# How far the row maxima run ahead, how they are turned, and where the hash bits stand in the matrix stream

## The chip, the cores and the metric

The kernel runs on one core of a Trainium2 chip. It is one program and one launch; the other cores are idle. The metric is the device time of one execution in microseconds, the median of several runs. A profiled execution is taken beside them; its trace gives every instruction of the engines: TensorE (PE, with its weight loads as PEld), VectorE (DVE), ScalarE (ACT), GpSimd (POOL), and the issues of transfers on SyncE's queue (SP).

## The reference

Two parts follow each other: attention over hash buckets, and a feed-forward layer.

```python
q_bits = (einsum('bhsd,dk->bhsk', q, proj) > 0)     # 6 bits; the same for k
mask = q_bucket[:, :, :, None] == k_bucket[:, :, None, :]
scores = where(mask, scale * q @ k.T, -1e9)
attn = exp(scores - max(scores)); attn /= sum(attn) + 1e-9
x = (attn @ v) arranged as [4*768, 8*64]
h = x @ w_in                                         # 512 -> 2048
g = where(h >= 1, h, where(h <= -1, 0, (h + 1)**2 / 4))
out = g @ w_out                                      # 2048 -> 512
```

There are 4 batches of 8 heads, 768 positions and head width 64, all in float32. A query and a key may only meet if all six signs of their projections agree.

## The kernel before, in words

**Pairs and phases.** Two heads make a pair; there are 16 pairs. Queries are handled in halves of 384 columns, so attention is a sequence of 32 phases: phase 2p is the first half of pair p, phase 2p+1 its second. A phase has six score steps (`s_step`, lines 324 and 328), one for each block of 128 keys. A step computes the transposed scores of both heads into a slot of PSUM (three products for the precision, line 324, and one with the mask rows, line 328), and ScalarE writes their exponentials (line 330). At the end of the phase come the output products with the values (`pv_group`, line 375, two groups of three key blocks) and the sums of the exponentials over the keys: GpSimd adds three blocks each (`sum_part`, line 339), and four small products with ones finish the sum of the phase before (`sum_mm`, line 349, into the bank aux; `sum_put` copies it on ScalarE, line 362, and stores it).

**Mask rows.** For each pair the tile `MB` holds rows of the hash bits. The product of these rows over queries and keys (line 251 and line 328) adds a large negative number where bits differ. One more row holds, for each query, the negated maximum of its scores, so that line 328 also subtracts the maximum. The hash bits of pair p+2 are made in one of pair p's phases: `bits_mm` (line 211, four products of 32 output rows into one bank), `bits_cmp` (VectorE), `bits_scale` (ScalarE), and `bits_put`, eight small transfers on SP's queue (line 238).

**Maxima.** The row maximum must be known before the phase that needs it. So each phase also computes untransposed scores of later phases: a maximum (`max_mm`, lines 248 and 251) is one block of 128 queries against half of the keys, for both heads, into a slot; `max_red` (line 261) reduces it on VectorE into a column of a tile `nr`. Six maxima make one phase's rows. Phases 1 to 6 do seven each, so from phase 7 on the maxima run a full phase further ahead than at the start.

**Turning.** The maxima stand in columns and are needed as a row. There are two ways. `row_first` (line 290, six products of 97 output rows, a copy on ScalarE, two one-row operations on VectorE, line 300) stands between the two groups of output products; it serves the rows of phases 1 to 7. `half_turn` (line 268, four products of 67 output rows in the 64-row shape that the maxima have) stands behind the sixth maximum of a phase; `half_put` takes the smaller of both halves on VectorE (line 277) and sends the row into `MB` with two transfers on SP's queue (line 283), and a copy to memory with two more (line 285). It serves phases 8 to 31, in the phase ahead of each.

**Order.** All order is written by hand: an engine runs its instructions in program order. A string gives the order of maxima (M) and score steps (s) within a phase and the slot of each; `PLAIN` outside of phases 8 to 26, `CLOSE` within. Slots 0 to 2 have two banks each; a fourth is made of the output bank and aux.

```python
PLAIN = "MMsMsMsMsMss", (0, 1, 2, 3, 0, 1, 2, 3, 0, 1, 2, 0)
CLOSE = "MMsMssMsMsMs", (0, 1, 2, 3, 0, 1, 2, 0, 3, 1, 2, 0)
```

Work at the end of a phase is collected in bursts by place: 0 and 1 before the output products, 3 between their two groups, 2 behind them. In phases 3 to 26 VectorE and ScalarE also prepare weights for the second part there (lines 69 to 82), with a bank of slot 1 as scratch. SP's queue is in order too: it issues each transfer once what it waits for is done. In phases 28 to 31 VectorE and GpSimd prepare the first columns of x for the feed-forward layer (lines 634 to 639), and in phases 30 and 31 VectorE does the additions of line 339 as well.

**Feed-forward.** From 408.9 us on, PE computes the two matrix products (lines 757, 894 and 989); the change doesn't touch that part.

Of the kernel before, what the change touches and what calls it, by code (L numbers as in the profile page):

```python
# [25 lines left out]
NJ = S // P  # L26
# [85 lines left out]
ADDS = (0, 1, 3, 4)  # L112
DIRECT, VSUM = 1, 58
AHEAD0 = (0, 2, 3, 4, 5, 6)
AT = 5
WORD, TURN, TFIRST = 1, 2, True
PLAIN = "MMsMsMsMsMss", (0, 1, 2, 3, 0, 1, 2, 3, 0, 1, 2, 0)
CLOSE = "MMsMssMsMsMs", (0, 1, 2, 3, 0, 1, 2, 0, 3, 1, 2, 0)
C0, C1 = 8, 27
# [2 lines left out]
def order(ph):  # L122

    return CLOSE if C0 <= ph < C1 else PLAIN


def turns(ph, kind):

    return [t for x, t in zip(*order(ph)) if x == kind]


def ahead(ph, j):

    seen = [i for i, x in enumerate(order(ph)[0]) if x == "s"]
    return order(ph)[0][:seen[j]].count("M")
# [3 lines left out]
def attention(ctx, tc, wst, T1, T2, qk, v, pj, cv, x_d, s_d, n_d, tasks, shared):  # L139
# [6 lines left out]
    slots = [psum.tile([P, 2, 512], F32, name=f"s{i}") for i in range(3)]  # L146
    obank = psum.tile([P, 512], F32, name="o")
    aux = psum.tile([P, 512], F32, name="aux")
    shared["word"] = slots[WORD][:, 0].bitcast(I32)
    slots = [[t[:, 0], t[:, 1], t] for t in slots] + [[obank, aux]]  # L150
# [92 lines left out]
    def max_mm(pr, i, kh, ps):  # L243
        qr, mb = QR(pr), MB(pr)
        its = slice(i * P, (i + 1) * P)
        smax[pr, i, kh] = ps
        for h in range(2):
            nc.tensor.matmul(out=ps[h][:, 0:HS], lhsT=qr[64 * h:64 * h + 64, 0, its],  # L248
                             rhs=qr[64 * h:64 * h + 64, 1, halves[kh]], start=True, stop=False)
        for h in range(2):  # L250
            nc.tensor.matmul(out=ps[h][:, 0:HS], lhsT=mb[64 * h:64 * h + 33, 0, its],  # L251
                             rhs=mb[64 * h:64 * h + 33, 1, halves[kh]], start=False, stop=True)

    def max_red(pr, i, kh):
        hf = i // NG
        nr = NR[(2 * pr + hf) % 3]
        ps = smax.pop((pr, i, kh))
        c = 32 + i % NG
        for o, x in ([(nr[:, kh, c::64], ps[2][:, :, 0:HS])] if len(ps) > 2
                     else [(nr[:, kh, c + 64 * h:c + 64 * h + 1], ps[h][:, 0:HS]) for h in range(2)]):  # L260
            nc.vector.tensor_reduce(out=o, in_=x, axis=AX.X, op=ALU.max, negate=True)  # L261

    def half_turn(pr, hf, ps):
        nr = NR[(2 * pr + hf) % 3]
        for kh in range(2):
            for h in range(2):
                r = slice(64 * h, 64 * h + 64)
                nc.tensor.matmul(out=ps[h][0:TW, HS + 64 * kh:HS + 64 * kh + 64], lhsT=nr[r, kh, 32:32 + TW],
                                 rhs=ident_r[r, r], start=True, stop=True, skip_group_check=True)
        te = small.tile([TW, P], F32R, name="te")  # L270
        halfs[pr, hf] = te, ps[2][0:TW, :, HS + 64:HS + P]
        nc.scalar.copy(out=te.rearrange("p (h n) -> p h n", h=2), in_=ps[2][0:TW, :, HS:HS + 64])

    def half_put(pr, hf):
        te, other = halfs.pop((pr, hf))
        tv = te.rearrange("p (h n) -> p h n", h=2)
        nc.vector.scalar_tensor_tensor(out=tv, in0=tv.bitcast(F32), scalar=CLAMP, in1=other, op0=ALU.min, op1=ALU.min)
        b, sl = 2 * pr // H, halves[hf]
        for o in (None, n_d[b]):
            for h in range(2):  # L280
                t = te[64 * h:64 * h + NG].bitcast(F32)
                if o is None:
                    nc.sync.dma_start(out=MB(pr)[64 * h + 7:64 * h + 8, 0, sl].bitcast(F32), in_=t)
                else:
                    nc.sync.dma_start(out=o[2 * pr % H + h:2 * pr % H + h + 1, sl], in_=t)
# [48 lines left out]
    def sum_part(gr, n):  # L334
        p = [PT[(NG * gr + i) % NP_][:, :, 0:HS] for i in range(NG)]
        eng = nc.vector if gr >= VSUM else nc.gpsimd
        if n == 0:
            sums[gr] = work.tile([P, 2, HS], F32, name="part", bufs=2)
        eng.tensor_tensor(out=sums[gr], in0=sums[gr] if n else p[0], in1=p[n + 1], op=ALU.add)  # L339
# [11 lines left out]
    def sum_last(gr):  # L351

        for i in range(NG):
            for k in range(2):
                for h in range(2):
                    r = NW * (2 * h + k)
                    nc.tensor.matmul(out=aux[r:r + NW, 0:HS], lhsT=ones, rhs=pts[NG * (gr + k) + i][:, h, 0:HS],
                                     start=(i == 0), stop=(i == NG - 1), skip_group_check=True)
# [33 lines left out]
    def keep_rows(n):  # L392

        for _ in range(n):
            for h in range(2):
                r = slice(64 * h, 64 * h + 64)
                nc.tensor.matmul(out=(obank, aux)[h][:, 0:2 * P], lhsT=idle[r, 0:P], rhs=idle[r],
                                 start=True, stop=True)
# [59 lines left out]
    events, mids, bursts = defaultdict(list), defaultdict(list), defaultdict(list)  # L458

    def burst(ph, place, fn, *a):  # L460
        bursts[ph, place].append((fn, a))
# [9 lines left out]
    k = 0  # L471
    last, halves_of = {}, {}
    for ph in range(NPH):
        for m in range(7 if 0 < ph < 7 else NJ):
            q, i = 1 + k // NJ, k % NJ
            if q < NPH:
                events[ph].append((q // 2, q % 2 * NG + i // 2, i % 2, slots[turns(ph, "M")[m] if m < NJ else WORD]))
                last[q] = ph
            k += 1
    for q in range(1, NPH):  # L480
        ph = last[q]
        if ph == q - 1:
            burst(ph, 3, row_first, q // 2, q % 2, slots[TURN])
        else:
            halves_of[ph + 1] = q // 2, q % 2
    for pr in range(NPAIR):
        if pr + 2 < NPAIR:
            if pr > 0:
                mids[NU * pr - 4].append((load_qk, (pr + 2,)))
            ph = 2 * pr + (pr == 0)  # L490
            burst(ph, 0, bits_mm, pr + 2)
            burst(ph, 1, bits_cmp, pr + 2)
            burst(ph, 1, bits_scale, pr + 2)
            burst(ph, 1, bits_put, pr + 2)
            for t in range(2):
                burst(ph, 1, round_qk, pr + 2, t)
                mids[NJ * ph + NJ + 2 + 2 * t].append((low_qk, (pr + 2, t)))
        if pr + 1 < NPAIR:
            mids[NU * pr + 3].append((load_v, (pr + 1,)))

    def run(l):
        for fn, a in l:
            fn(*a)

    made = defaultdict(int)

    def maxima(ph, upto):
        while made[ph] < min(upto, max(NJ if ph in halves_of else 0, len(events[ph]))):
            m = made[ph]
            made[ph] += 1  # L510
            turned = m == AT and ph in halves_of
            if m < len(events[ph]):
                a = events[ph][m]
                max_mm(*a)
                if turned:
                    half_turn(*halves_of[ph], a[3])
                max_red(*a[:3])
            elif turned:
                half_turn(*halves_of[ph], slots[turns(ph, "M")[m]])
            if turned:  # L520
                half_put(*halves_of[ph])

    NF_ = NS // NJ
    for ph in range(NF_ + 1):
        for j in range(NJ):
            n = NJ * ph + j
            if n < NS:
                maxima(ph, ahead(ph, j) if ph else AHEAD0[j])
                if n == 1:
                    keep_rows(4)  # L530
                s_step(n)
                if n == 0:
                    keep_rows(4)
            if 0 < ph < NF_ - DIRECT + 1 and j in ADDS:
                k = ADDS.index(j)
                sum_part(2 * ph - 2 + k // 2, k % 2)
            run(mids.pop(n, ()))
            if j < NJ - 1:
                for k in range(2):
                    run(tasks.pop(2 * n + k, ()))  # L540
        maxima(ph, NJ + 1)
        run(bursts.pop((ph, 0), ()))
        run(bursts.pop((ph, 1), ()))
        run(tasks.pop(2 * (NJ * ph + NJ - 1), ()))
        if NF_ - DIRECT <= ph < NF_:
            sum_last(2 * ph)
            sum_put(2 * ph)
        if ph < NF_:
            pv_group(2 * ph)
            run(bursts.pop((ph, 3), ()))  # L550
            pv_group(2 * ph + 1)
        if TFIRST:
            run(bursts.pop((ph, 2), ()))
        if 0 < ph < NF_ - DIRECT + 1:
            sum_mm(2 * ph - 2)
            sum_put(2 * ph - 2)
        run(bursts.pop((ph, 2), ()))
        run(tasks.pop(2 * (NJ * ph + NJ - 1) + 1, ()))
    assert not bursts and not pts and not sums, (events, bursts)
    for g in sorted(tasks):  # L560
# [659 lines left out]
```

## Time and profile before

| | us |
|---|---|
| median of 3 runs | 926.98 (926.97 to 927.6) |
| profiled execution | 927.48 |
| span of its trace | 925.7 |
| PE busy | 917.5 |
| DVE busy | 666.4 |
| ACT busy | 524.9 |
| POOL busy | 313.2 |
| first product of the feed-forward layer | 408.90 |

The granted clock of TensorE is 1.000 through the whole span. A busy PE isn't PE at its peak, since the ends of matmuls are modelled; what counts is the distance between the starts of its instructions. The profiled execution's time is its span and 1.8 us around it.

### The profile page before, as it was taken

To read this page: it belongs to the slowest core of one execution; us is meant where nothing else is said; L and a number is where in the kernel's file an instruction comes from. 1 tells how busy PE (TensorE), PEld (TensorE's weight loads), DVE (VectorE), ACT (ScalarE), POOL (GpSimd) and SP (SyncE) were. 2 spreads that over 40 slices of the span, in tenths; PEclk is the share of its full clock that TensorE was granted. 3 is DMA by queue.
4 is the path that set the end of the run, shared out by engine and by line. 5 is a ranking of instruction groups with operands and counts; after the bars stand their busy time and mean duration, and the time that the engine had idled before them with its cause. 6 is when DMAs were issued, how large, how long until landed. Compare 5 with 4: busy or idle time off the path is not lost.

```text
span 925.7 us, 17069 instructions
## 1 busy us (share of the span) xinstructions
PE 917.5 (99%) x6217; PEld 733.1 (79%) x6217; DVE 666.4 (72%) x1167; ACT 524.9 (57%) x895; POOL 313.2 (34%) x222
## 2 busy tenths in 40 slices
PE   9999999999999999999999999999999999999998
PEld 6667766666666666669999888889889889888986
DVE  6578877777777776849987877876857777655564
ACT  4556666666666665546565555464654545644444
POOL 5588788777878888640000000000000000000000
PEclk9999999999999999999999999999999999999999
DMA  2233334444444433553944789865395654644421
GB/s 89 93 120 132 119 115 139 145 142 142 146 145 141 143 124 102 147 150 133 318 165 137 249 275 292 268 184 158 105 265 150 187 149 122 186 114 116 124 80 68
DMA packets 91412, 142.96 MB, mean 154 GB/s; under 512 B 14288, under 2 KB 53056, under 8 KB 91328
## 3 DMA queue, kind: packets, MB, share of 16 engines
q1 hardware_dynamic: 91040, 141.87, 49.7%
q8 instruction: 49, 0.80, 0.4%
q14 instruction: 35, 0.29, 0.1%
q10 hardware_dynamic: 288, 0.01, 0.0%
HBM read 106.23 MB, written 34.06 MB: 152 GB/s over the span
## 4 chain that ended last, share of the span: by engine, by line
PE 95%; DVE 2%; ACT 1%; DMA 1%; SPq 1%; issue 0%; ACTq 0%; DVEq 0%
PE y L757 28%; PE h L989 19%; PE o L375 14%; PE s L324 11%; PE h L894 7%; PE s L328 3%; PE s L248 3%; PE aux L349 2%; PE s L251 2%; PE aux L211 1%; PE o L248 1%; PE o L251 1%; PE s L290 1%; PE aux L390 0%; DVE nr L261 0%; DMA t<-ed 0%
## 5 line engine op out<-in xcount | busy, mean ns | idle before, releaser
L330 ACT ACTIVATE p<-s 128x768 f32<-128x768 f32 x192 | 155.5, 814 | 59.7 <-PE s L328 55.8
L261 DVE TENSOR_REDUCE nr<-s 128x2 fp32r<-128x768 f32 x132 | 123.2, 956 | 77.2 <-PE s L251 52.1
L722 DVE SCALAR_TENSOR_TENSOR t<-t 128x384 f32<-128x384 f32 x128 | 71.3, 557 | 103.5 <-ACT z L717 103.4
L375 PE MATMUL o<-p,vraw 128*64 128x384 f32 (+1 forms) x768 | 132.8, 491 | 0.0
L339 POOL TENSOR_TENSOR part<-p,p 128x768 f32<-128x768 f32 x58 | 107.1, 1846 | 68.1 <-PE aux L349 67.8
L757 PE MATMUL y<-t,ghi 128*128 128x512 f32 x384 | 124.6, 395 | 0.5 <-ACT ghi L727 0.5
L375 PEld LDWEIGHTS o<-p,vraw 128*64 128x64 f32 x768 | 51.6, 136 | 69.1 <-issue 64.6
L339 POOL TENSOR_TENSOR part<-part,p 128x768 f32<-128x768 f32 x58 | 98.4, 1696 | 3.6
L324 PE MATMUL s<-t,t 64*128 64x384 f32 x768 | 98.4, 333 | 0.0
L727 ACT CAST ghi<-z 128x384 fp32r<-128x384 f32 x129 | 65.1, 505 | 29.9 <-DVE z L723 26.1
L989 PE MATMUL h<-wbig,t 128*128 128x384 f32 x399 | 81.4, 336 | 0.0
L717 ACT ACTIVATE z<-t,m 128x384 f32<-128x384 f32 x128 | 79.0, 617 | 4.2
L757 PEld LDWEIGHTS y<-t,ghi 128*128 128x128 f32 x384 | 71.3, 188 | 11.7 <-ACT ghi L727 0.9
L716 ACT ACTIVATE t<-h,mh 128x384 f32<-128x384 f32 x56 | 32.6, 582 | 83.9 <-PE h L894 45.9
L757 PE MATMUL y<-t,glo 128*128 128x512 f32 x192 | 76.0, 396 | 0.0
L757 PE MATMUL y<-woh,glo 128*128 128x512 f32 x192 | 75.7, 394 | 0.2
L989 PEld LDWEIGHTS h<-wbig,t 128*128 128x128 f32 x399 | 71.6, 188 | 5.2
L757 PE MATMUL y<-woh,ghi 128*128 128x512 f32 x192 | 75.5, 393 | 0.0
L757 PE MATMUL y<-wol,ghi 128*128 128x512 f32 x192 | 75.5, 393 | 0.0
L723 DVE TENSOR_TENSOR z<-t,z 128x384 f32<-128x384 f32 x128 | 71.4, 558 | 4.6
L324 PE MATMUL s<-t 64*128 64x384 f32 x384 | 71.1, 365 | 1.2 <-ACT p L330 0.9
L731 DVE TENSOR_TENSOR glo<-z,ghi 128x384 fp32r<-128x384 f32 x128 | 70.5, 550 | 0.2 <-ACT ghi L727 0.2
(192 smaller groups left out, 1815.2 us busy)
## 6 DMA issues: line engine op xcount, KB each, us to landing
t<-wc SPq DMA_DIRECT2D x92, 256.0 KB
wraw<-wc SPq DMA_DIRECT2D x76, 256.0 KB
qk<-in_qk_dram SPq DMA_DIRECT2D x15, 768.0 KB
wraw<-in_w_in_dram SPq DMA_DIRECT2D x16, 512.0 KB
wraw<-in_w_out_dram SPq DMA_DIRECT2D x16, 512.0 KB
t<-ed SPq DMA_DIRECT2D x36, 192.0 KB
xd<-xs SPq DMA_DIRECT2D x16, 385.0 KB
vraw<-in_v_dram SPq DMA_DIRECT2D x16, 384.0 KB
```

The source lines that it names most:

```text
L261: nc.vector.tensor_reduce(out=o, in_=x, axis=AX.X, op=ALU.max, negate=True)
L324: nc.tensor.matmul(out=ps[h][:, 0:HS], lhsT=k[r, 1, ks], rhs=q[r, 0, sl], start=(k is hi and q is hi), stop=False)
L330: nc.scalar.activation(out=p[:, :, 0:HS], in_=ps[2][:, :, 0:HS], func=AF.Exp, scale=SCALE)
L339: eng.tensor_tensor(out=sums[gr], in0=sums[gr] if n else p[0], in1=p[n + 1], op=ALU.add)
L375: nc.tensor.matmul(out=obank[64 * h:64 * h + 64, 0:w], lhsT=vraws[pr][:, j, h, :], rhs=p[:, h, 0:w], start=(j == 0), stop=(j == NJ - 1), s ...
L717: nc.scalar.activation(out=z, in_=t, func=AF.Relu, scale=1.0, bias=m1)
L722: nc.vector.scalar_tensor_tensor(out=t, in0=t, scalar=1.0, in1=t, op0=ALU.min, op1=ALU.mult)
L723: nc.vector.tensor_tensor(out=z, in0=t, in1=z, op=ALU.add)
L727: nc.scalar.copy(out=g[0], in_=g[2])
L731: nc.vector.tensor_tensor(out=g[1], in0=g[2], in1=g[0].bitcast(F32), op=ALU.subtract)
L757: nc.tensor.matmul(out=ys[c][m], lhsT=g_[:, m * P:(m + 1) * P], rhs=w, start=(first and k == 0), stop=(last and k == 2))
L989: nc.tensor.matmul(out=ps, lhsT=w[:, cs], rhs=x, start=(n == 0 and s not in (2, 3, 6)), stop=(n == 5), skip_group_check=True)
```

## The change

Four things are edited.

- The maxima: phases 1 to 3 do seven, all others six (`LEADS = 3`). So three are done ahead rather than six, and phase 30, which had none, does the last three.
- The turning: `row_first` serves phases 1 to 3 only; from the row of phase 4 on `half_turn` is used. In phase 3 it stands behind the seventh maximum (`at_of`), elsewhere behind the sixth place as before.
- The hash bits: from phase 4 on `bits_mm` stands behind the output products and directly ahead of the row sums, and writes the second bank of slot 2 in place of aux. `bits_cmp`, `bits_scale` and `bits_put` follow it there (place 4). The rounding of the pair's queries and keys stays where it was.
- The switch `TFIRST`, which has no use any more, is gone, and where no maximum is left to share a slot with, the turn takes slot 1 (`WORD`).

```diff
-AT = 5
-WORD, TURN, TFIRST = 1, 2, True
+LEADS = 3
+WORD, TURN, HASH = 1, 2, 2
...
-        for m in range(7 if 0 < ph < 7 else NJ):
+        for m in range(NJ + (0 < ph <= LEADS)):
...
-        ph = last[q]
-        if ph == q - 1:
-            burst(ph, 3, row_first, q // 2, q % 2, slots[TURN])
+        if q > 3:
+            halves_of[q - 1] = q // 2, q % 2
         else:
-            halves_of[ph + 1] = q // 2, q % 2
+            burst(last[q], 3, row_first, q // 2, q % 2, slots[TURN])
...
-            burst(ph, 0, bits_mm, pr + 2)
-            burst(ph, 1, bits_cmp, pr + 2)
-            burst(ph, 1, bits_scale, pr + 2)
-            burst(ph, 1, bits_put, pr + 2)
+            burst(ph, 2 * (ph > 2), bits_mm, pr + 2, slots[HASH][1] if ph > 2 else aux)
+            for fn in (bits_cmp, bits_scale, bits_put):
+                burst(ph, 4 if ph > 2 else 1, fn, pr + 2)
...
+    def at_of(ph):
+
+        return NJ if ph <= LEADS else NJ - 1
+
     def maxima(ph, upto):
-        while made[ph] < min(upto, max(NJ if ph in halves_of else 0, len(events[ph]))):
+        while made[ph] < min(upto, max(at_of(ph) + 1 if ph in halves_of else 0, len(events[ph]))):
             m = made[ph]
             made[ph] += 1
-            turned = m == AT and ph in halves_of
+            turned = m == at_of(ph) and ph in halves_of
...
             elif turned:
-                half_turn(*halves_of[ph], slots[turns(ph, "M")[m]])
+                half_turn(*halves_of[ph], slots[WORD])
...
-        if TFIRST:
-            run(bursts.pop((ph, 2), ()))
+        run(bursts.pop((ph, 2), ()))
+        run(bursts.pop((ph, 4), ()))
         if 0 < ph < NF_ - DIRECT + 1:
             sum_mm(2 * ph - 2)
             sum_put(2 * ph - 2)
-        run(bursts.pop((ph, 2), ()))
```

## The prediction

> **What bounds the kernel now.** I read the page's busy shares and its chain of waits first, then the places of the output products (line 375, one stretch per phase) in that chain, and last the timelines of TensorE, VectorE, ScalarE and the DMA queue around one hash phase and around phases 29 to 31.
>
> ```profile
> PE 917.5 (99%) x6217; PEld 733.1 (79%) x6217; DVE 666.4 (72%) x1167; ACT 524.9 (57%) x895; POOL 313.2 (34%) x222
> PE 95%; DVE 2%; ACT 1%; DMA 1%; SPq 1%; issue 0%; ACTq 0%; DVEq 0%
> ```
>
> The matrix engine is busy 99% of the span and makes up 95% of the chain. So an edit counts by what it takes from PE's stream or by a hole that it puts into it; idle time elsewhere is free. Phase lengths can be read from the chain as the distance between successive line 375 rows (the first of each phase):
>
> ```profile
> 77.69 2.09 PE o L375 x12
> ...
> 90.45 2.10 PE o L375 x12
> ...
> 104.00 2.08 PE o L375 x12
> ...
> 116.42 4.04 PE o L375 x24
> 128.86 4.02 PE o L375 x24
> 140.50 4.04 PE o L375 x24
> ```
>
> These are phases 4 to 9. Up to phase 6 the products are cut in two (x12) by a row turn; from phase 7 on they are whole (x24). Phase 5 lasts 90.45 - 77.69 = 12.76 us and phase 6 13.55 (it holds hash products, phase 5 doesn't). Phase 7 has 12.42, phase 8 (hash) 12.44, phase 9 (none) 11.64.
>
> **Part 1: rows in row tiles, one maximum fewer.** Phases 4 to 6 lose their seventh maximum and their row turn and get the small turn that phases 8 and 9 have already. So phase 5 should come to phase 9's length (12.76 - 11.64 = 1.12) and phases 4 and 6 to phase 8's (13.55 - 12.44 = 1.11 each): 3.34. Phase 7 loses the row turn that phase 6 had left in its interval: 12.42 - 11.64 = 0.78. Phase 3 keeps seven maxima and gains a small turn, which takes
>
> ```profile
> 127.04 0.25 PE L268 MATMUL s<-ident_r,nr 64*67 64x64 f32 x4
> ```
>
> 0.25 us at most, so -0.2. Together 3.34 + 0.78 - 0.2: **3.9 us** less in the first eight phases. Each turned row also brings three more transfers (four instead of one) on SP's queue in phases 3 to 6 and takes two one-row VectorE operations away; neither is on the path there. In phase 3 ScalarE's copy of the turned rows stands behind two exponentials and the weight operations of VectorE behind it, in the bank of the next phase's second maximum; PE's output products (4.0 us) cover that, about to the tenth. If the cover fails it costs a few tenths once.
>
> **Part 2: hash products between output products and row sums** (12 phases, 4 to 26).
>
> ```profile
> 128.01 0.85 PE L211 MATMUL aux<-qk,pw 128*32 128x384 f32 x8
> 128.79 4.09 PE L375 MATMUL o<-p,vraw 128*64 128x384 f32 x24
> 132.81 0.85 PE L349 MATMUL aux<-part,ones 128*32 128x384 f32 x8
> 133.59 0.45 PE L248 MATMUL s<-t 64*128 64x384 f32 x2
> ...
> 134.05 0.34 PE L248 MATMUL s<-t 64*128 64x384 f32 x2
> ...
> 134.41 0.34 PE L324 MATMUL s<-t 64*128 64x384 f32 x2
> ...
> 135.12 0.34 PE L248 MATMUL o<-t 64*128 64x384 f32 x1
> ...
> 402.00 2.14 PE L357 MATMUL aux<-p,ones 128*32 128x384 f32 x24
> 404.07 1.19 PE L375 MATMUL o<-p,vraw 128*64 128x386 f32 x6
> ```
>
> Hash products and row sums have one shape (128 rows, 32 columns). Alone, eight instructions of it cost 0.78 (128.01 to 128.79), and the hash phase is 12.44 - 11.64 = 0.80 longer. The last sums put 24 of them in a row: 2.07, so each further eight cost (2.07 - 0.78) / 2 = 0.645. Put next to the sums, the hash should cost 0.645: 0.155 x 12 = 1.9 saved. The row's bank and weights don't change between its groups, as here they would, so the lower end is nothing saved; a loss has no row, because the stream loses one change of shape and gains none. I take **1.6**, near the row of the same shape.
>
> The new order adds waits. VectorE's compare now waits for the end of the hash products; behind it are only the next phase's first reductions, which come later anyway. Bank 1 of slot 2 must be free of the compare before the next phase's first scores (134.41, some 1.6 after the hash ends; the compare and its hand-over take 0.7). ScalarE's copy of the row sums now stands behind the scaling of the bits, and frees aux for the third maximum (135.12):
>
> ```profile
> 128.95 0.55 DVE L216 TENSOR_SCALAR bits<-aux 128x384 fp32r<-128x384 f32 x1
> ...
> 129.53 0.71 ACT L219 ACTIVATE bits<-bits,cvt 128x384 fp32r<-128x384 f32 x1 [0.54 <-DVE bits L216]
> ...
> 133.80 0.48 ACT L362 COPY rows<-aux 128x384 f32<-128x384 f32 x1 [0.35 <-PE aux L349]
> ```
>
> In phase 8 the products would start at 128.01 and last 4.02; hash until 132.9, compare and scale until 134.3, the copy until 134.8, against 135.0: hidden, with 0.2 to spare. Without that it would cost a tenth or two per hash phase.
>
> **Part 3: three maxima move to phase 30.** One costs 134.41 - 134.05 = 0.36; three are contained in part 1's gain and come back here.
>
> ```profile
> 380.87 4.11 PE L375 MATMUL o<-p,vraw 128*64 128x386 f32 x24
> ...
> 385.69 0.44 PE L324 MATMUL s<-t 64*128 64x384 f32 x2
> ...
> 386.83 0.44 PE L328 MATMUL s<-t 33*128 33x384 f32 x1 [0.19 <-DMA t<-te]
> ...
> 391.79 4.09 PE L375 MATMUL o<-p,vraw 128*64 128x384 f32 x24
> ```
>
> Phase 30 has no maxima before, and PE has holes in it: 0.3 for a row's transfer (386.83) and about as much twice for exponentials. The maxima (1.08) would fill these and cost 0.3 if that were all. But the small turn for phase 31 needs the reductions of these maxima, which until now were done a phase earlier, and VectorE has its own work in front:
>
> ```profile
> 385.86 1.37 DVE L339 TENSOR_TENSOR part<-p,p 128x768 f32<-128x768 f32 x1 [0.81 <-PE aux L349]
> 387.15 0.54 DVE L637 TENSOR_TENSOR qk<-qk,t 128x384 f32<-128x384 f32 x1
> 387.73 0.36 DVE L639 CAST t<-qk 128x384 fp32r<-128x384 f32 x1
> ...
> L261 DVE TENSOR_REDUCE nr<-s 128x2 fp32r<-128x768 f32 x132 | 123.2, 956 | 77.2 <-PE s L251 52.1
> ```
>
> First maximum done 386.4, two reductions of 0.96, a sum (1.37 in its row; I allow 0.95, as the reduction of as many elements), 0.54, 0.36 and the third reduction in two halves (0.96): 391.0, where PE would be there at 390.0. Turn, two scores and change take 1.7: products at 392.7 to 393.0 instead of 391.79. **+1.1**, bounds +0.3 (reductions in time) and +2.0 (another 0.9 on VectorE, as its 1.37 shows possible).
>
> **Part 4: what the hash rows push back on SP's queue.** No term of the diff, but the one that worries me most.
>
> ```profile
> 131.37 5.46 SPq L238 DMA_DIRECT2D t<-bits  x8
> ...
> 138.03 0.37 SPq L187 DMA_DIRECT2D qk<-in_qk_dram  x1
> ...
> 141.51 1.45 SPq L283 DMA_DIRECT2D t<-te  x2
> ...
> 162.11 0.37 SPq L187 DMA_DIRECT2D qk<-in_qk_dram  x1
> ```
> ```profile
> 143.00:144.00 1.00, 1.00 (x8) 0.43 (x6) 0.80 (x2) 0.00 (x0) 1.00 (x1) 1.00 0.78 212
> ...
> 166.00:167.00 1.00, 1.00 (x8) 0.43 (x6) 0.93 (x3) 0.05 (x1) 1.00 (x2) 1.00 0.93 381
> 167.00:168.00 1.00, 1.00 (x8) 0.43 (x6) 0.80 (x2) 0.00 (x0) 1.00 (x1) 1.00 0.06 19
> ```
> ```profile
> 146.58 0.34 PE L328 MATMUL s<-t 33*128 33x384 f32 x2
> ...
> 170.64 0.34 PE L328 MATMUL s<-t 33*128 33x384 f32 x2
> ```
>
> Eight hash rows hold SP for 5.46 us; behind them are the stores and loads of a weight block and a pair, and then the turned row (te) that the next even phase's first line 328 needs. Part 2 lets the hash rows start at 134.3 instead of 131.37, so all behind them comes 2.95 later. The loads, which kept the DMA engines busy (next to last column) until about 143.8 and 167.0, then end at 146.7 and 169.95. The row itself is ready at 141.5 and is now issued behind loads that are still moving. How long it takes with idle engines:
>
> ```profile
> 384.25 1.55 SPq L283 DMA_DIRECT2D t<-te  x2
> 386.40:386.50 0.10, 0.10 (x3) 0.00 (x0) 0.10 (x1) 0.00 (x0) 0.01 (x1) 1.00 0.06 15
> ```
>
> its second half moves at 386.45 and PE goes on at 386.83, nearly 0.4 later. If the row can't pass the loads, it lands at 147.1 in phase 9 and 170.3 in phase 11; it is needed at 146.45 and 170.5 (0.13 earlier than before by part 2). So 0.6 late in phases 9, 17 and 25, which load sums too, and just in time in the eight other odd phases. If it passes them, nothing is late. I take **+1.5**; bounds 0 and 11 x 0.6 = 6.6.
>
> The Trainium skill (DMA: Bandwidth & Descriptors, section "Queues, rings and completion order") has a rule that speaks against the change here: each DMA engine consumes the descriptors of a ring in order, so a small row would stay behind a large load of its queue. By that rule part 4 is paid; without it the sum below would be 1.5 better. No row here shows a row waiting behind loads, or passing them.
>
> **Sum.** -3.9 - 1.6 + 1.1 + 1.5 = -2.9. The profiled execution took 927.48 us (925.7 span and 1.8 around it), 0.5 above the median of 926.98; 927.48 - 2.9 = 924.6 in its terms, and **924.1** as a median.
>
> **Rivals.**
> - *Rows are never late* (part 4 is nothing): -4.4, 922.6. For it: the even margins of 0.2; against: the loads ahead in the one queue, some five microseconds of it.
> - *A little late everywhere*: at 0.4 in each of the 11 odd phases the gain is eaten: -4.4 + 4.4, 927.0. The eight phases with 0.2 to spare are near enough.
> - *Hash gains nothing and phase 30 pays 2.0*, so the change moves work without its main effect: -3.9 + 2.0 + 1.5, 926.6. For it: VectorE's slow operations around 385; against: line 357's row.
> - *Slower: the turned row stuck behind the loads.* Place: the first line 328 of each even phase. Price 0.6 in all 11, 6.6: -4.4 + 6.6 = +2.2, 929.2. It decides from 0.4 per phase on, which needs loads 0.6 slower than 167.0 shows, or a DMA engine that lags behind the mean share.
>
> **How the numbers follow.** 0.2% is 1.85 us, about what a measurement of this kernel can tell from no change. Forecast 40% (923 to 925.1), never late 20%, a little late 14%, hash nothing 14%, slower 12%. Faster 0.60, same 0.28, slower 0.12. The range for eight in ten is 921.6 (parts 2 and 3 at their good ends, nothing late: -3.9 - 1.9 + 0.3 = -5.5) to 927.8 (the two cases near no change with the measurement's spread); the forecast's own is 923 to 925.1.
>
> **What would show it.** Part 1: line 290 falls from 42 to 18 instructions and line 268 rises from 96 to 112; phases 4 to 7 by the chain near 12.3, 11.6, 12.3, 11.6. Part 2: from the hash row to the sums 0.65, hash phases 12.3. Part 3: products of phases 29 and 30 some 12 apart, and a wait of line 268 for the reductions. Part 4: line 328 waiting for te in phases 10, 18 and 26. The forecast is wrong if even phases show that wait throughout, or none, or if line 248's third maximum waits for ScalarE's copy.

## The result, and the profile after

The changed kernel takes 931.67 us (five executions, 929.87 to 933.18) against 926.97 for the kernel before (926.53 to 927.6). The ratio is 1.0051 with an interval of 1.0035 to 1.0067: it is slower by 4.7 us, where I had forecast 2.9 less. The profiled execution took 933.18 us, 931.4 of them span (925.7 before).

First the lines of the changed kernel's page that answer to those shown of before: busy times, the chain's shares by engine, and one group of instructions.

```profile
PE 917.2 (98%) x6209; PEld 734.9 (79%) x6209; DVE 664.3 (71%) x1164; ACT 521.9 (56%) x895; POOL 312.5 (34%) x222
PE 85%; DMA 7%; SPq 3%; DVE 3%; ACT 1%; issue 1%; ACTq 0%; DVEq 0%
L328 PE MATMUL s<-t 33*128 33x384 f32 x384 | 72.7, 340 | 6.1 <-DMA t<-te 5.6
```

PE is no less busy in microseconds (917.2 against 917.5), but its share of the chain falls from 95% to 85%; DMA and SP's queue now hold 10%. The last line says what for: line 328 waits for the turned row (`t<-te`). These waits are listed again under PE's weight loads, since a weight load stands ahead of each product; the two figures are one wait and are not added. Before, TensorE waited for such a row once, 0.2 us at 386.83.

The chain of waits of the changed kernel, from the products of phase 4 to the row for phase 10, and the products of phase 26 (start, length, what ran):

```profile
75.68 4.02 PE o L375 x24
89.54 5.41 DMA t<-te
...
141.61 3.64 DMA t<-te
...
289.12 4.78 DMA t<-te
...
349.44 4.02 PE o L375 x24
```

A turned row's transfer stands in the chain once ahead of each even phase from 6 to 26, eleven times. It takes 3.2 to 5.4 us from its issue to its landing (3.6 to 5.4 in the rows shown), and PE's next product begins as it lands. So the row of each even phase comes late, not three of eleven.

Around one of these, phases 8 and 9, TensorE does this (start, length, instruction, tile, shapes, count, wait in brackets):

```profile
125.82 4.09 PE L375 MATMUL o<-p,vraw 128*64 128x384 f32 x24
129.84 0.85 PE L211 MATMUL s<-qk,pw 128*32 128x384 f32 x8
130.51 0.83 PE L349 MATMUL aux<-part,ones 128*32 128x384 f32 x8
131.27 0.44 PE L248 MATMUL s<-t 64*128 64x384 f32 x2
...
143.89 0.51 PE L324 MATMUL s<-t,t 64*128 64x384 f32 x4
145.29 0.62 PE L328 MATMUL s<-t 33*128 33x384 f32 x2 [0.89 <-DMA t<-te]
```

The first four lines show that the hash move itself did what it was to do: from hash to sums 0.67, from sums to the next shape 0.76, together 1.43 where the two took 0.78 each before. The last two show what it cost: line 328 begins 1.4 us after the four products of line 324 begin, instead of 0.35 (before, 146.23 and 146.58).

SP's queue in the same stretch, and what the DMA engines did (next to last column: their mean busy share):

```profile
132.09 5.45 SPq L238 DMA_DIRECT2D t<-bits  x8
...
138.74 0.37 SPq L187 DMA_DIRECT2D qk<-in_qk_dram  x1
...
141.61 1.46 SPq L283 DMA_DIRECT2D t<-te  x2
```
```profile
144.00:145.00 1.00, 0.40 (x6) 0.08 (x2) 1.00 (x2) 0.11 (x1) 1.00 (x2) 1.00 0.58 137
```

The hash rows go out 6.3 us after the output products begin, then the pair (768 KB) and right behind it, at 139.17, the weight block (512 KB), then the row (two transfers of 1.5 KB). A share of 0.58 in this stretch means that the engines are full until about 144.6, and the row lands at 141.61 + 3.64 = 145.25.

Phase 30, which got the three maxima:

```profile
395.81 0.25 PE L268 MATMUL s<-ident_r,nr 64*67 64x64 f32 x2 [0.63 <-DVE nr L261]
```
```profile
385.79 4.04 PE o L375 x24
...
397.54 4.02 PE o L375 x24
```

The turn's second half waits for the reductions, and the phase takes 397.54 - 385.79 = 11.75 instead of 10.92.

### The profile page after: what moved, and what is told of

It reads as the page before. It is cut to its first block, busy times and chain, and to the rows that moved or that the text cites. A ratio compares the mean times of both kernels' runs of the same rounds, so it can differ in the third digit from the quotient of the medians.

```text
span 931.4 us, 17037 instructions
## 1 busy us (share of the span) xinstructions
PE 917.2 (98%) x6209; PEld 734.9 (79%) x6209; DVE 664.3 (71%) x1164; ACT 521.9 (56%) x895; POOL 312.5 (34%) x222
## 4 chain that ended last, share of the span: by engine, by line
PE 85%; DMA 7%; SPq 3%; DVE 3%; ACT 1%; issue 1%; ACTq 0%; DVEq 0%
PE y L758 28%; PE h L990 18%; PE o L375 10%; PE s L324 8%; PE h L895 7%; DMA t<-te 5%; PE s L328 3%; PE s L248 2%; PE s L251 2%; PE aux L349 1%; SPq L238 1%; PE s L211 1%; DMA t<-ed 1%; PE o L251 1%; DVE nr L261 1%
## 5 line engine op out<-in xcount | busy, mean ns | idle before, releaser
L324 PE MATMUL s<-t,t 64*128 64x384 f32 x768 | 102.1, 333 | 0.0
L328 PE MATMUL s<-t 33*128 33x384 f32 x384 | 72.7, 340 | 6.1 <-DMA t<-te 5.6
L324 PE MATMUL s<-t 64*128 64x384 f32 x384 | 74.7, 364 | 0.7 <-ACT p L330 0.4
```

The costliest lines, as they stand in the source:

```text
L324: nc.tensor.matmul(out=ps[h][:, 0:HS], lhsT=k[r, 1, ks], rhs=q[r, 0, sl], start=(k is hi and q is hi), stop=False)
L328: nc.tensor.matmul(out=ps[h][:, 0:HS], lhsT=mb[r, 1, ks], rhs=mb[r, 0, sl], start=False, stop=True)
```

## The experiments

The theory after the result: parts 1 to 3 brought about what I had worked out, and the late row alone makes the kernel slower. The hash rows, moved behind the output products, push the pair's and the weights' loads back on SP's queue, and the row behind them can't land before they end. Its rivals: the row is late because its issue is late (a matter of the instructions ahead of it on SP, not of their bytes); or the cause isn't the hash move at all, but the maxima or the turn.

**The change without the hash move.** Lines 490 to 492 get back the places and the bank of before; the rest stays as changed.

```diff
-            burst(ph, 2 * (ph > 2), bits_mm, pr + 2, slots[HASH][1] if ph > 2 else aux)
+            burst(ph, 0, bits_mm, pr + 2)
             for fn in (bits_cmp, bits_scale, bits_put):
-                burst(ph, 4 if ph > 2 else 1, fn, pr + 2)
+                burst(ph, 1, fn, pr + 2)
```

> The changed kernel with the hash products, compare, scaling and hash rows back at their old place (ahead of the output products, bank aux); maxima and turning as changed. Theory (the late hash rows hold SP, the loads come later and the turned row waits behind them): no wait of line 328 for te, so only parts 1 and 3 are left: -3.9 + 0.8 (phase 30 measured) = 923.9. Rival A (the small turn with three maxima ahead is what makes rows late, wherever the hash stands): the wait stays, about 11 us in the even phases, 933. Rival B (the row waits only because SP issues it late, not because of the loads): no wait either, 923.9.

Measured: 923.94 us (923.61 to 924.19), ratio 0.9968 (0.9956 to 0.998) against 926.86 for the kernel before on the same chip. PE waits for no row's transfer. The output products in the chain of this kernel, phases 3 to 8 and 26:

```profile
64.01 4.04 PE o L375 x24
76.41 4.02 PE o L375 x24
88.00 4.04 PE o L375 x24
100.39 4.02 PE o L375 x24
111.98 4.04 PE o L375 x24
...
124.39 4.02 PE o L375 x24
...
340.62 4.02 PE o L375 x24
```

Phases 4 to 7 take 12.40, 11.59, 12.39 and 11.59. So parts 1 and 3 are a gain of 2.9 by themselves, as the theory has it, and the late row comes with the hash move.

**The hash move alone, on the kernel before.**

```diff
-            burst(ph, 0, bits_mm, pr + 2)
-            burst(ph, 1, bits_cmp, pr + 2)
-            burst(ph, 1, bits_scale, pr + 2)
-            burst(ph, 1, bits_put, pr + 2)
+            burst(ph, 2 * (ph > 2), bits_mm, pr + 2, slots[2][1] if ph > 2 else aux)
+            for fn in (bits_cmp, bits_scale, bits_put):
+                burst(ph, 2 if ph > 2 else 1, fn, pr + 2)
```

> The kernel before with the hash products, compare, scaling and hash rows moved behind the output products, nothing else. Theory: rows of phases 10 to 26 (nine even ones) wait behind the loads as in the changed kernel, about 1.0 us each, and the hash saves 0.14 x 12 = 1.7: 927.0 - 1.7 + 9 = 934. Rival A: no waits, 925.3.

Measured: 935.99 us (935.25 to 937.15), ratio 1.01 (1.0085 to 1.0115): 9.1 slower than the kernel before, with neither the maxima nor the turn touched. Its waits on TensorE (us in all, times, longest):

```profile
PE s L328 <- DMA t<-te: 4.9, 8, 1.1
```

It is the same wait, and it isn't alone. By the distances between the output products the ten even phases from 8 to 26 (I had expected nine late rows) are together 9.2 longer than in the run with both loads behind the row, below. In phases 4 and 6 the moved hash products wait 0.5 each themselves: in phase 4 line 300 still reads the bank of the row turn, which is now theirs too, until 80.89 + 1.12 = 82.01, and they begin at 82.12. So phases 4 to 7, where no row is late, take 0.9 more than before instead of 0.3 less. In the changed kernel that turn is gone from these phases.

**The changed kernel with both loads behind the row.** The load of a pair two further on goes from four steps ahead of a pair's start to one, and the constant that places the weight blocks' loads from -6 to -2 steps.

```diff
-WLOAD = -6
+WLOAD = -2
...
-                mids[NU * pr - 4].append((load_qk, (pr + 2,)))
+                mids[NU * pr - 1].append((load_qk, (pr + 2,)))
```

> The changed kernel, but the loads of the next pair and of the next weight block are put behind the turned row in the odd phases' program (and the weight load behind it in the even ones); same bytes. Theory: the row goes out once it is ready, with only a 256 KB store ahead, no wait of line 328: -3.9 - 1.6 + 0.8 = -4.7, 922.3. Rival A: waits stay, 931.7. Rival B: the row goes out at once too, 922.3.

Measured: 921.55 us (921.22 to 922.34), ratio 0.9945 (0.9929 to 0.9962). That is 10.1 less than the changed kernel and 5.3 less than the kernel before: it beats both. SP's queue in phase 9, and places of the chain:

```profile
128.88 5.42 SPq L238 DMA_DIRECT2D t<-bits  x8
...
137.97 1.52 SPq L283 DMA_DIRECT2D t<-te  x2
...
140.38 0.36 SPq L187 DMA_DIRECT2D qk<-in_qk_dram  x1
```
```profile
63.39 4.04 PE o L375 x24
75.00 4.02 PE o L375 x24
...
98.83 4.02 PE o L375 x24
...
122.68 4.02 PE o L375 x24
134.94 4.04 PE o L375 x24
146.57 4.02 PE o L375 x24
...
337.68 4.02 PE o L375 x24
```

The hash rows are where the change put them, only the loads have changed places with the row, and the waits are gone. This prices them: from the products of phase 4 to those of phase 26 it is 349.44 - 75.68 = 273.76 in the changed kernel and 337.68 - 75.00 = 262.68 here, 11.1 us or 1.0 on average for each of the eleven rows; by the starts of line 375 in TensorE's timeline the single even phases lose between 0.5 (phase 20) and 1.5 (phase 18). (That is the profiled execution, the slowest of five; between the medians it is 10.1.) Phase 9 takes 12.26 and phase 10 takes 11.63: the hash costs 0.63 where the run without the move has 0.81 (phases 4 and 5). From phase 8 to 26 this kernel takes 215.00 and that one 340.62 - 124.39 = 216.23; a ninth of the difference, 0.14, is what one hash move saves. (The medians of the two differ by 2.4 rather than 12 x 0.14 = 1.6; in the profiled executions 0.6 of the difference lies ahead of phase 0, whose products begin at 24.77 there and at 24.16 here.)

**The row on ScalarE's queue.** The two transfers of line 283 are issued by ScalarE after its last exponential of the phase, and SP's queue is left as changed. Lines of this kernel are shifted by two (330 for 328).

```diff
-                    nc.sync.dma_start(out=MB(pr)[64 * h + 7:64 * h + 8, 0, sl].bitcast(F32), in_=t)
+                    rows_out.append((MB(pr)[64 * h + 7:64 * h + 8, 0, sl].bitcast(F32), t))
...
         maxima(ph, NJ + 1)
+        while rows_out:
+            o, t = rows_out.pop(0)
+            nc.scalar.dma_start(out=o, in_=t)
```

> The changed kernel, but the two transfers of the turned row are issued from ScalarE's queue behind the phase's last exponential; hash rows and loads stay on SP as changed. Issue is then no longer late. Theory in its narrow form (order within one queue): the row passes the loads and lands some 2.5 us after its issue, no waits, 922.3 plus what 1.4 us of ScalarE per phase cost (it has the room: 0). Theory in its wide form (each DMA engine works off what came first, whatever the queue): the row still lands with the end of the loads, waits of about 1 us in the even phases stay, 931. Rival B (issue alone): no waits, 922.3.

Measured: 944.46 us (941.03 to 947.18), ratio 1.0188 (1.0163 to 1.0214). It is neither figure, since two costs came on top that I hadn't foreseen. ScalarE's timeline in phases 9 and 11, the chain in phase 11, one of TensorE's waits, and TensorE behind it (third figure from the end: the granted clock):

```profile
137.53 5.10 ACTq L548 DMA_DIRECT2D t<-te  x2
142.73 0.66 ACT L69 ACTIVATE wsq<-wraw 128x512 f32<-128x512 f32 x1 [6.79 <-DMA wraw<-in_w_in_dram]
...
167.06 1.40 ACTq L548 DMA_DIRECT2D t<-te  x2
```
```profile
167.06 5.55 DMA t<-te
```
```profile
PE s L248 <- DVE wsq L82: 10.1, 3, 3.8
```
```profile
146.00:148.00 2.00, 2.00 (x16) 2.00 (x16) 0.98 (x3) 0.81 (x1) 2.00 (x3) 0.50 0.98 314
```

In phase 9 the issue alone held ScalarE for 5.10 us; ScalarE's part of the weight preparation (line 69) then came late, VectorE's line 82 behind it, and the bank that PE needed. (The bracket names a load, but in the changed kernel line 69 of this phase ran at 138.96, before that load was issued at 139.17; the chain runs over the issue.) The same happens in phases 17 and 25, with issues of 3.97 and 4.61; in the other eight odd phases from 5 to 23 the issue takes 1.40. The moving loads aren't the whole reason: in phase 11 the pair's load goes out at 166.83, just ahead of the row, and the issue takes 1.40 all the same. What sets phases 9, 17 and 25 apart is that SP issues the loads of sums there too, and that the row's issue begins 15.0 to 15.1 us after the output products instead of 12.6 to 14.2; which of the two matters this run doesn't tell.

The second cost is the clock. After the wait of 3.83 that ended at 144.23 it was 0.50 for some five microseconds, and 1.00 again from 152. The two other waits, 2.82 and 3.45, were followed by 0.50 too. Together the waits and the slow stretches make phases 10, 18 and 26 longer by 17.7 than with both loads behind the row.

The question of the run is answered by the other phases. The row is late in six of the even ones, 12, 14, 16, 20, 22 and 24 (5.5 together), although no load is ahead of it in its queue. In phase 11 its issue took 1.40, so it wasn't drawn out, and the row landed 5.55 after it, not the 2.5 of the narrow form. So the order within SP's queue isn't all that holds the row: once the loads move, it stays behind them from another issuer too, and not only at its issue. In phases 5 and 7, where it was issued ahead of the loads, it came in time.

**One load behind the row, the other ahead.** Two runs of the changed kernel with half of the edit of the run with both: the pair's load alone (`NU * pr - 1`), and the weight block's alone (`WLOAD = -2`).

> The changed kernel with only the load of the next pair (768 KB) put behind the turned row in odd phases; the weight store and load (256 + 512 KB) stay ahead of it. Theory (the row lands when the bytes ahead of it are through): half of the bytes are ahead, they are through some 2.5 us sooner, and the row lands in time: no waits, about 922.5. Rival B (the wait comes from SP's late issue of the row): the row is issued only about 0.5 us sooner, so half of the 1.0 us per even phase stays: 927.

> The changed kernel with only the weight loads (512 KB) put behind the turned row; the pair's 768 KB and the store of 256 KB stay ahead of it. Theory: two thirds of the bytes are ahead and through some 1.8 us sooner, about 0.5 us before the row is needed; waits in few phases at most (those that also load sums), 922 to 924. Rival B: 927.

Measured: 922.25 us (921.88 to 922.42), ratio 0.9948 (0.993 to 0.9965), and 922.12 us (921.36 to 922.38), ratio 0.9945 (0.9927 to 0.9962). In neither does PE wait for a row's transfer. Phase 9 with the pair ahead and the weights behind (SP's queue, the DMA engines, TensorE):

```profile
136.51 0.38 SPq L187 DMA_DIRECT2D qk<-in_qk_dram  x1
...
139.04 1.52 SPq L283 DMA_DIRECT2D t<-te  x2
```
```profile
140.00:141.00 1.00, 1.00 (x12) 0.38 (x14) 0.00 (x0) 0.57 (x2) 0.15 (x2) 1.00 0.55 137
```
```profile
142.05 0.34 PE L328 MATMUL s<-t 33*128 33x384 f32 x2
```

The row is issued 3.0 us before PE needs it; in the changed kernel it was 2.6 (141.61, and line 328 due at about 144.25). Those 0.4 are not the 1.0 that was lost. What differs is the loads' end: here about 140.5, 1.5 ahead of the need, there 144.6, 0.35 after it. Phase 21 rules out that the issue alone decides. There the run with the pair ahead sends the row at

```profile
281.21 1.49 SPq L283 DMA_DIRECT2D t<-te  x2
```

and line 328 begins at 285.37, in time, 4.16 later. In the changed kernel the row was issued at 289.12, 4.5 ahead of the need at 293.64, so with more time in hand, and line 328 began 0.3 late, at 293.94. So the bytes ahead of the row decide, and late issue is no more than a part. Taking away either load is enough, since each is worth more than what was missing.

**Six maxima ahead instead of three**, on the kernel with both loads behind the row.

```diff
-LEADS = 3
+LEADS = 6
```

> The kernel with the loads behind the row, and maxima six ahead again (seven in phases 1 to 6, none in phase 30); rows still turned in the small way from phase 4 on, hash products behind the output products. It takes part 3 alone away. Phase 30 should fall from 11.7 back to 10.9 us and its wait of line 268 should go, while phases 4 to 6 each gain one maximum of 0.36: +1.08 - 0.83, 921.8 against 921.55, within the spread.

Measured: 922.58 us (922.22 to 923.29), ratio 0.9953 (0.9937 to 0.9969). The chain's output products around phases 4 to 6 and phase 30:

```profile
63.72 4.04 PE o L375 x24
...
100.55 4.02 PE o L375 x24
...
376.10 4.04 PE o L375 x24
...
387.02 4.02 PE o L375 x24
```

Phase 30 is back at 10.92 (from 11.74 in the run with three ahead), 0.8 less. Phases 4 to 6 take 100.55 - 63.72 = 36.83 together, with three ahead 98.83 - 63.39 = 35.44: 1.4 more, so that a maximum there costs 0.46 and not the 0.36 that I had reckoned with. I had expected 0.25 more in all. The net of 0.6 in favour of three ahead agrees in sign with the 1.0 between the two medians. These were taken in two sittings and their ranges overlap slightly (up to 922.34, from 922.22), so more can't be said of so small a size.

## Why the prediction was wrong

The step that failed is the size of **Part 4**: "Eight hash rows hold SP for 5.46 us" and what stands behind them. The mechanism was named there, and the rival *Slower: the turned row stuck behind the loads* is what happened, with its place, the first line 328 of each even phase. I took +1.5 (bounds 0 and 6.6); it was 11.1 in the profiled execution and 10.1 between medians, beyond the upper bound. That bound multiplied by eleven the lateness worked out for one phase, 0.6, and an even phase lost up to 1.5.

- *The row can't pass the loads*: right, which the prediction had left open. The Trainium skill (DMA: Bandwidth & Descriptors, "Queues, rings and completion order") lets each DMA engine consume a ring's descriptors in order. The row that landed 0.65 us after the loads' end in phase 9 agrees. The Trainium skill (DMA: Bandwidth & Descriptors, "Issuing engines are not separate DMA queues") says that transfers of another issuer run on the same 16 engines, and that this saves only the time of the issue. The run with the row on ScalarE agrees, with 5.55 us to the landing, though its issue wasn't small.
- *Phase 9, 0.6 late.* The hash rows' start was right (6.27 after the products begin, 6.29 in the working), and so was the loads' end (18.8 against 18.7). The row took some 0.65 from there instead of the 0.4 that I had read where engines were idle, so it landed 1.0 late rather than 0.6, and PE lost a little more as it began again (the pair of line 328 took 0.62, not 0.34). Phases 10, 18 and 26 are 1.35, 1.54 and 1.21 longer than in the run with both loads behind the row: 4.1 instead of the 1.8 of the working (taken as 1.5).
- *"Just in time in the eight others"*: wrong, and the larger part of the error: these eight lost 7.0 together, 0.5 to 1.35 each. I had moved the loads' end by the hash rows' shift alone. For phase 11, the hash place of the kernel before, and of the changed kernel the products, the row's wait, the pair's issue and the DMA engines:

```profile
152.08 0.85 PE L211 MATMUL aux<-qk,pw 128*32 128x384 f32 x8
```
```profile
151.06 4.09 PE L375 MATMUL o<-p,vraw 128*64 128x384 f32 x24
...
170.49 0.66 PE L328 MATMUL s<-t 33*128 33x384 f32 x2 [0.86 <-DMA t<-te]
```
```profile
164.38 0.37 SPq L187 DMA_DIRECT2D qk<-in_qk_dram  x1
```
```profile
169.00:170.00 1.00, 0.63 (x8) 0.31 (x4) 1.00 (x2) 0.33 (x1) 1.00 (x1) 1.00 0.69 240
```

  From the start of the output products, the pair was to be issued at 162.11 + 2.95 - 152.08 = 13.0 and is at 13.3; the loads were to end at 169.95 - 152.08 = 17.9. In steps finer than the row shown the engines are full until 169.3 and half busy from there to 170, so the end is known to some tenths only: 18.2 to 18.6. The row was to land at 18.2, and PE goes on at 19.4, where it could have at 18.6. So the loads' end, 0.4 to 0.7 out, more than uses up a margin of 0.2, and the landing after them, as in phase 9, does the rest. The pair's later issue explains 0.3 of it; whether the loads themselves took longer (4.9 to 5.3 from the pair's issue, 4.9 in the working) can't be told from this.
- *Part 1, -3.9*: right. Line 268 rises to 112 instructions and line 290 falls to 18, as its group in the changed kernel shows:

```profile
L290 PE MATMUL s<-ident_r,nr 128*97 128x128 f32 x18 | 2.2, 258 | 0.0
```

  In the run without the hash move, phases 4 to 7 take 47.97 together, where the working had 2 x (12.44 + 11.64) = 48.16: 0.2 better.
- *Part 2, -1.6*: right in size, 0.14 x 12 = 1.6, and right that one shape next to the other saves (0.67 measured for 0.645 in the row of the last sums, but 0.76 for the sums themselves). The third maximum didn't wait for ScalarE's copy.
- *Part 3, +1.1*: 0.8 measured (11.75 against 10.92), with the wait where it was put, at line 268.
- *Sum.* Measured terms for the profiled execution: -3.9 - 0.2 - 1.6 + 0.8 + 11.1 = +6.2, against a span longer by 5.7. With the 10.1 between medians it is +5.2, against +4.7. Of the half that is left over, 0.14 lies ahead of phase 0, whose products begin at 24.83 instead of 24.97, and 0.1 in phase 3, whose turn cost 0.07 and not 0.2; the rest I don't account for. Without Part 4 the terms give -4.9, and the run with both loads behind the row measured -5.3.

The rival had 12%, because I took the margins of 0.2 in eight phases for safe. They were differences of shifts of several microseconds, each known to some tenths, and one error in them counted in all eight at once.

## What to carry to other kernels

When an edit moves small transfers later on a queue, follow what stands behind them in that queue up to its landing, and compare it with its need in every period; a small row behind a megabyte of loads lands with the loads. Where the row is due sooner than the loads, let it go out first: two constants here turned a loss of 4.7 us into a gain of 5.3. And bound a repeated wait by the number of periods times what a plausible error of its inputs would make of it, not by the one period in which it shows.

## What the runs showed of the hardware

- A row (two transfers of 1.5 KB) issued on SP's queue behind 1.25 MB of loads landed 3.2 to 5.4 us after its issue at eleven places; with idle engines PE went on 2.6 after it (384.25 to 386.83, before). The landing was about 0.65 after the loads' end in phase 9 and 1.4 in phase 17; in most other phases the engines stay full with what stands behind the row, and the end can't be read.
- Issued by ScalarE instead, the row landed 5.55 us after its issue in phase 11. I had expected another issuer to be free of that queue.
- Issuing these two transfers took ScalarE 1.40 us in eight phases and 5.10, 3.97 and 4.61 in three. The Trainium skill (DMA: Bandwidth & Descriptors, "Issuing engines are not separate DMA queues") calls the time of an issue usually small relative to the transfer itself. Here it is not.
- TensorE's granted clock fell to 0.50 after waits of 2.82, 3.45 and 3.83 us in the run with the row on ScalarE. In the changed kernel, with waits of up to 0.9, it stayed at 1.00.
- The first two products of line 328 behind a wait took 0.62 us together, against 0.34 in an unbroken stream, with the clock still granted at 1.00.
